# Top-k attention, mixture of experts and feed-forward on one core: fewer, longer score lists, a sign in place of a clipped excess, and PSUM in two pools

## The chip, the cores and the metric

The kernel runs on one core of one Trainium2 chip. The metric is the device time of one execution in microseconds (us), as the median of several runs. A profile of one more execution shows each engine's instructions: TensorE (PE, with its weight loads as PEld), VectorE (DVE), ScalarE (ACT), GpSimd (POOL) and SyncE (SP), which starts most of the transfers.

## What is computed

The reference runs three stages one after the other; all data are f32.

```python
# attention: 2 batches, 8 heads, 576 rows, 64 wide
scores = (1 / np.sqrt(64)) * np.matmul(q, k.transpose(0, 1, 3, 2))
kth = np.partition(scores, -32, axis=-1)[..., -32:-31]
scores = np.where(scores >= kth, scores, -1e9)
attn = np.exp(scores - scores.max(-1, keepdims=True))
attn = attn / (attn.sum(-1, keepdims=True) + 1e-9)
x = np.matmul(attn, v)              # to 1152 tokens of 512
# experts: 8, each token to the one with the highest gate, at most 288 each
h = np.maximum(x_e @ w1[e], 0.0); y = gate * (h @ w2[e])
# feed-forward, 2048 wide
h = y @ w_in; out = (h * np.clip(h + 3, 0, 6) / 6) @ w_out
```

What matters here is the first mask: of each row's 576 scores only the 32 highest may count, so the kernel has to know each row's 32nd highest score exactly.

## The kernel before

The 1152 tokens are nine tiles of 128 rows; with eight heads that makes 72 units of 128 x 576 scores, here also called heads, numbered u. The attention stage is a loop over i that is written out as a software pipeline: in one turn each engine works for a different unit, and the letters of `STEP` (line 36) are the order within a turn. Each engine runs its own instructions strictly in the order in which they were recorded.

For one unit the steps are these. TensorE makes the scores in PSUM, and ScalarE's `fetch` (line 388) copies them to SBUF. `round1` (line 407): VectorE cuts the 576 scores into eight chunks of 72 and takes the eight highest of each with MAX8, into a list for each chunk. `excess` (line 413): GpSimd subtracts from each score its chunk's eighth highest. `cut_excess` (line 418): ScalarE takes the positive part of that, scaled by 2^64, so that only the seven highest of a chunk give something other than zero. `drop_excess` (line 421): GpSimd subtracts this from the scores, which leaves the scores without each chunk's first seven. `round2` (line 425): VectorE takes the eight highest of what is left, one MAX8 over 576. `merge` (lines 432 to 436): from nine lists of seven VectorE takes the 32 highest in order, by four MAX8 and three replacements between them; a replacement shows in the trace as a load of the values and the replacement itself. Then `shift` on GpSimd (line 454, the first 200 columns, 60 from unit 54 on, none for the last four) and `shift_rest` on ScalarE (line 459, the other columns) subtract from the highest score, `below` (line 463, ScalarE) marks what lies below the 32nd, TensorE transposes both into one PSUM tile, ScalarE takes the exponential (line 485), and TensorE multiplies with the values.

In turn i the three engines hold, each in this order: VectorE `round1` of unit i+1 dealt out with `merge` of unit i-3 by `interleave` (line 394), in some turns the normalisation of four heads (lines 503 and 504), then `round2` of unit i-2; GpSimd, after each eight units, `judge` for a tile (lines 442 to 445, four small instructions that keep what is needed to see later whether the lists sufficed), then `excess` of unit i, `shift` of i-3 and `drop_excess` of i-1; ScalarE `cut_excess` of i-1, `shift_rest` of i-3, `fetch` of i+3, `below` of i-3 and the exponential of i-4. In the last turns ScalarE also scales rows, and GpSimd sends them to the experts.

After attention come the eight experts on TensorE, each in 16 blocks of four products (line 1034), eight for the first layer (`hps`) and eight for the second (`yps`); their PSUM tiles all come from one pool of eight banks. Some turns into it, `check` (lines 961 to 980) works out on VectorE from what `judge` kept whether the fast pass may stand; if it may not, a slow pass of the whole computation follows. The last stage (lines 1141 and 1155) takes other PSUM pools once the experts' pool is given back. Results of an expert go from PSUM to SBUF in two halves, a rounded one by ScalarE (`x2h`, line 1051) and what is missing by VectorE (`x2l`, line 1052); the last stage's products read both.

Of the kernel before, what the change touches and what calls it, by code (L numbers as in the profile page):

```python
# [28 lines left out]
LOW = -3.4028234e38  # L29
NCK = 8  # L30
CW = S // NCK
KEEP = 7
PUSH = 2.0 ** 64
BIG = 2.0 ** 68
LEAST = 2.0 ** -32
# [26 lines left out]
def topk_attention_moe_ffn_kernel(ctx, tc, qT, kT, vx, vT, wg, w1, w2, w_in, w_out, out, cap):  # L62
# [20 lines left out]
    def forward(fast):  # L83
# [21 lines left out]
        sc = wp.tile([P, 2, E + 1], F32, name="sc")  # L105
        over = wp.tile([P, 2, NT, H, NCK], F32, name="over")
        rest_ok = wp.tile([P, 2, NT, H], F32, name="rest_ok")

# [138 lines left out]
        with ExitStack() as actx:  # L247
# [6 lines left out]
            if fast:  # L254
                lists = [big.tile([P, H, NCK + 1, KEEP + 1], F32, name=f"lists{i}") for i in range(2)]
            wg_sb = big.tile([P, HP, MC // E, E], F32, name="wg_sb")
# [77 lines left out]
            for i in range(2):  # L334
# [6 lines left out]
                lbufs.append(m)  # L341
            drop = big.tile([P, P], BF, name="drop")
            nc.vector.tensor_scalar(drop, ident, BIG, None, op0=OP.mult)

            def clear_rows(zero):
# [63 lines left out]
            def excess(u):  # L409
                t, h = divmod(u, H)  # L410
                st2[u] = wk.tile([P, S], F32, name="s2", bufs=3)
                s, s2 = (a.rearrange("p (c k) -> p c k", k=CW) for a in (st[u], st2[u]))
                nc.gpsimd.tensor_tensor(s2, s, lists[t % 2][:, h, :NCK, KEEP:].to_broadcast([P, NCK, CW]),  # L413
                                        op=OP.subtract)
# [12 lines left out]
            def merge(u):  # L427
                t, h = divmod(u, H)
                l = lists[t % 2][:, h, :, :KEEP]
                m = tops[t][:, h]  # L430
                l2 = wk.tile([P, NCK + 1, KEEP], F32, name="l2")
                yield lambda: nc.vector.max(m[:, 0:8], l)  # L432
                for i in range(1, 4):
                    yield lambda i=i: nc.vector.match_replace(out=l2, in_to_replace=m[:, 8 * i - 8:8 * i],  # L434
                                                              in_values=l if i == 1 else l2, imm_value=LOW)
                    yield lambda i=i: nc.vector.max(m[:, 8 * i:8 * i + 8], l2)  # L436

            def judge(t):

                l, thr = lists[t % 2], tops[t][:, :, TOPK - 1:]  # L440
                g = nc.gpsimd
# [399 lines left out]
        with ExitStack() as mctx:  # L841
# [56 lines left out]
            with ExitStack() as ectx:  # L898
                eb = ectx.enter_context(tc.tile_pool(name=of + "eb", bufs=2))
                ps = ectx.enter_context(tc.tile_pool(name=of + "ps", bufs=8, space=PS))  # L900
                xin, xe = {}, {}

                def two_banks():
                    return ps.tile([P, 2, 256], F32, tag="ps", name="xp2") if fast else None

# [17 lines left out]
                def turn_one(rows, x):  # L923
                    for k in range(HP):
                        xp = ps.tile([P, W], F32, tag="ps", name="xp1")
                        for r, a, n in rows:
# [34 lines left out]
                def check():  # L961

                    v = nc.vector
                    low = eb.tile([P, 3], F32, name="low", bufs=1)
                    hit = eb.tile([P, 3], BF, name="hit", bufs=1)
                    two = [over[:, i].rearrange("p a b c -> p (a b c)") for i in range(2)]
                    v.tensor_tensor(two[0], two[0], two[1], op=OP.max)
                    v.tensor_reduce(low[:, 0:1], two[0], axis=AX.X, op=OP.min)
                    v.tensor_reduce(low[:, 1:], rest_ok.rearrange("p k a b -> p k (a b)"), axis=AX.X, op=OP.min)
                    v.tensor_scalar(hit[:, 0:1], low[:, 0:1], 0.0, None, op0=OP.is_le)  # L970
                    v.tensor_scalar(hit[:, 1:2], low[:, 1:2], 0.0, None, op0=OP.is_lt)
                    v.tensor_scalar(hit[:, 2:], low[:, 2:], LEAST, None, op0=OP.is_lt)
                    hits = ps.tile([P, 3], F32, tag="ps", name="hits")
                    nc.tensor.matmul(hits, ones, hit, start=True, stop=True)
# [45 lines left out]
                def tokens_of_columns():  # L1020
                    who_is = ps.tile([P, 2, NT], F32, tag="ps", name="who_is")
                    for t in range(NT):
# [4 lines left out]
                class Expert:  # L1027
                    def __init__(self, x, col, w):
                        self.x, self.col, self.w, self.y = x, col, w, {}
                        self.h = eb.tile([P, NFF, W], F32, name="hT", bufs=2 if fast else 1)  # L1030
# [6 lines left out]
                    def use(self, wb, what):  # L1037
                        if what[0] == "a":
                            f = what[1]
                            o = ps.tile([P, W], F32, tag="ps", name="hps")[:, :self.w]  # L1040
                            yield from self.products(o, wb, self.x, True, True)
                            nc.scalar.activation(self.h[:, f, :self.w], o, AF.Relu)
                            return
                        d, half = what[1:]
                        if half == 0:
                            self.y[d] = ps.tile([P, W], F32, tag="ps", name="yps")[:, :self.w]
                        o = self.y[d]
# [32 lines left out]
                for m in range(E * NP):  # L1080
                    e, r = divmod(m, NP)
                    if r == 0:
                        ex = Expert(xe[e], lambda e=e: offv[e], Ws[e])
                    if r == OFR:
# [40 lines left out]
            if fast:  # L1125
                loaded.append(nc.values_load(again, min_val=0, max_val=P + 1))
            ps = mctx.enter_context(tc.tile_pool(name=of + "ps2", bufs=2, space=PS))
            mw = mctx.enter_context(tc.tile_pool(name=of + "mw", bufs=2))
            CH = 384
            NJ = CH // P  # L1130
            fw += [mw.tile([P, 2, 2, DM], F32R, name=f"fw{f}", bufs=1) for f in range(nearly, NF)]
            if not fast:
# [110 lines left out]
```

## Time and profile before

| what | us |
|---|---|
| median of 3 runs | 595.87 (595.73 to 596.02) |
| profiled execution | 595.49 |
| its span | 593.6 |
| TensorE busy | 558.6 |
| VectorE busy | 372.1 |
| ScalarE busy | 357.0 |
| GpSimd busy | 300.9 |

The span is what the profile shows from the first to the last instruction; the time of the execution is 1.9 us more. Busy times are for the whole span, and the stages differ: attention ends at about 236 us, the experts at about 385 us, and the last stage fills the rest. An instruction's length is from its start to the landing of its last result; the next one on the same engine often starts before that, so the distance between two starts is what an instruction costs its engine. The rows that are read more closely stand further down.

### The profile page before, as it was taken

Reading aid. Unit: us, or ns where it says so; the run is one execution under the profiler, and the core shown is the slowest. Engines: PE = TensorE matmul, PEld = TensorE weight load, DVE = VectorE, ACT = ScalarE, POOL = GpSimd, SP = SyncE. Lnnn points to the kernel's source line nnn. Section 1 sums busy time; section 2 is a strip of 40 time slices with the busy share of each in tenths; the row PEclk is TensorE's granted clock in tenths of the full one; section 3 lists DMA queues with packets and bytes.
Section 4 is the critical chain, followed back from the end, with each engine's and each line's share of the span. In section 5 each row is a group of like instructions: output and inputs, shape, how many; then the busy total and the mean of one; then the engine's idle time right before and its main releaser. Section 6 shows DMA issues by size and latency. Waiting matters only on the chain.

```text
span 593.6 us, 13628 instructions
## 1 busy us (share of the span) xinstructions
PE 558.6 (94%) x4831; PEld 489.1 (82%) x4831; DVE 372.1 (63%) x1774; ACT 357.0 (60%) x689; POOL 300.9 (51%) x375
## 2 busy tenths in 40 slices
PE   8999998888878879999999999999999999999994
PEld 4777776666666668999999999998989999998993
DVE  6999999999999997103534344366666663222230
ACT  5999999999989995111345434455555542242221
POOL 8999999999989995100223223234223340040002
PEclk9999999999999999999999999999999999999998
DMA  8639100000008002874897978323222300020001
GB/s 257 213 130 316 56 20 2 22 2 2 2 2 315 26 19 99 340 282 162 319 352 278 358 281 323 105 70 105 75 72 71 108 1 1 2 106 1 1 1 58
DMA packets 18260, 73.49 MB, mean 124 GB/s; under 512 B 2543, under 2 KB 3183, under 8 KB 16007
## 3 DMA queue, kind: packets, MB, share of 16 engines
q1 hardware_dynamic: 16743, 67.81, 32.0%
q0 software_dynamic: 1440, 4.72, 2.0%
q8 instruction: 40, 0.66, 0.4%
q14 instruction: 37, 0.30, 0.2%
HBM read 63.09 MB, written 9.44 MB: 122 GB/s over the span
## 4 chain that ended last, share of the span: by engine, by line
PE 62%; DVE 32%; POOL 3%; issue 1%; ACT 1%; DVEq 0%; POOLq 0%; ACTq 0%
PE h L1141 17%; PE acc L1155 16%; PE hps L1034 12%; PE yps L1034 12%; DVE lists L407 11%; DVE lists L425 7%; DVE l L434 6%; DVE tops L436 4%; DVE tops L432 1%; DVE x_tok L504 1%; PE xp L167 1%; PE av L497 1%; POOL s L413 1%; POOL s L421 1%; PE pt L656 1%
## 5 line engine op out<-in xcount | busy, mean ns | idle before, releaser
L407 DVE MAX8 lists<-s 128x8 f32<-128x72 f32 x576 | 119.1, 221 | 3.1 <-ACT s L391 2.8
L1141 PE MATMUL h<-x2h,fw 128*128 128x384 f32 x384 | 98.2, 337 | 1.1 <-DVE x2l L1052 1.1
L421 POOL TENSOR_TENSOR s<-s,cut 128x576 f32<-128x576 f32 x72 | 92.5, 1285 | 0.1
L478 PE MATMUL pt<-ident,ub 128*128 128x128 f32 x350 | 69.7, 285 | 21.5 <-ACT pts L485 17.4
L1155 PE MATMUL acc<-fw,gh 128*128 128x512 f32 x288 | 89.5, 392 | 0.0
L413 POOL TENSOR_TENSOR s<-s,lists 128x576 f32<-128x576 f32 x72 | 84.2, 1170 | 4.9 <-DVE lists L425 2.8
L478 PEld LDWEIGHTS pt<-ident,ub 128*128 128x128 f32 x350 | 49.0, 140 | 43.4 <-issue 15.3
L1034 PE MATMUL yps<-hT,wslot 128*128 128x192 f32 (+5 forms) x512 | 78.5, 302 | 0.0
L497 PE MATMUL av<-vt,pts 128*64 128x96 f32 x1440 | 75.2, 250 | 1.0 <-DVE eids L240 1.0
L1141 PEld LDWEIGHTS h<-x2h,fw 128*128 128x128 f32 x384 | 70.1, 188 | 5.1 <-DVE x2l L1052 1.3
L1034 PEld LDWEIGHTS yps<-hT,wslot 128*128 128x128 f32 x512 | 72.5, 190 | 0.6
L1034 PE MATMUL hps<-xe,wslot 128*128 128x192 f32 (+5 forms) x512 | 72.5, 302 | 0.6 <-ACT xe L173 0.6
L1034 PEld LDWEIGHTS hps<-xe,wslot 128*128 128x128 f32 x512 | 71.2, 190 | 0.9 <-ACT xe L173 0.9
L497 PEld LDWEIGHTS av<-vt,pts 128*64 128x64 f32 x1440 | 61.8, 135 | 12.2 <-issue 9.3
L1141 PE MATMUL h<-x2l,fw 128*128 128x384 f32 x192 | 64.6, 336 | 0.0
L479 PE MATMUL pt<-drop,lb 128*128 128x128 bf16 x350 | 63.2, 219 | 0.0
L1144 ACT ACTIVATE g<-h,three 128x384 f32<-128x384 f32 x48 | 27.9, 582 | 55.3 <-PE h L1141 55.0
L1145 DVE SCALAR_TENSOR_TENSOR g<-g,h 128x384 f32<-128x384 f32 x48 | 26.5, 552 | 54.0 <-ACT g L1144 53.7
L1155 PEld LDWEIGHTS acc<-fw,gh 128*128 128x128 f32 x288 | 53.4, 188 | 8.2
L463 ACT ACTIVATE lb<-s,tops 128x576 bf16<-128x576 f32 x71 | 57.0, 803 | 4.0 <-DVE tops L436 3.9
L1149 DVE TENSOR_TENSOR gl<-g,gh 128x384 fp32r<-128x384 f32 x48 | 27.4, 572 | 50.2 <-ACT gh L1148 50.2
L1148 ACT CAST gh<-g 128x384 fp32r<-128x384 f32 x48 | 24.6, 513 | 56.8 <-PE acc L1155 52.1
(462 smaller groups left out, 1049.5 us busy)
## 6 DMA issues: line engine op xcount, KB each, us to landing
wslot<-in_w_dram SPq DMA_DIRECT2D x15, 2048.0 KB, 8.7
raw<-in_w_in_dram SPq DMA_DIRECT2D x16, 512.0 KB, 3.5
raw<-in_w_out_dram SPq DMA_DIRECT2D x16, 512.0 KB, 5.5
xs<-x_tok SPq DMA_DIRECT2D x8, 576.0 KB, 10.1
vt<-in_vx_dram SPq DMA_DIRECT2D x8, 365.0 KB, 3.4
vts<-in_vT_dram SPq DMA_DIRECT2D x8, 288.0 KB, 4.6
qt<-in_qT_dram SPq DMA_DIRECT2D x8, 256.0 KB, 4.8
wslot<-in_w_dram SPq DMA_DIRECT2D x2, 1024.0 KB
```

Of the source, the lines that this page charges most:

```text
L407: yield lambda c=c: nc.vector.max(lists[t % 2][:, h, c], st[u][:, c * CW:(c + 1) * CW])
L413: nc.gpsimd.tensor_tensor(s2, s, lists[t % 2][:, h, :NCK, KEEP:].to_broadcast([P, NCK, CW]), op=OP.subtract)
L421: nc.gpsimd.tensor_tensor(st2[u], st[u], cuts.pop(u), op=OP.subtract)
L425: nc.vector.max(lists[t % 2][:, h, NCK], st2.pop(u))
L434: yield lambda i=i: nc.vector.match_replace(out=l2, in_to_replace=m[:, 8 * i - 8:8 * i], in_values=l if i == 1 else l2, imm_value=LOW)
L463: nc.scalar.activation(lbufs[u % 2][:, :S], st.pop(u), AF.Relu, bias=tops[t][:, h, TOPK - 1:], scale=-1.0)
L478: nc.tensor.matmul(pt[:, c], ubufs[u % 2][:, cs], ident, is_transpose=True, start=True, stop=False)
L479: nc.tensor.matmul(pt[:, c], lbufs[u % 2][:, cs], drop, start=False, stop=True)
L497: nc.tensor.matmul(av[t, g][rows, h % 4], pts[:, c, rows], vt[b, h // 2][:, at:at + VC], start=c == 0, stop=c == 4)
L1034: nc.tensor.matmul(out, wb[:, k], m[:, k, :self.w], start=first and k == 0, stop=last and k == HP - 1)
L1141: nc.tensor.matmul(h2, fw[f][:, 0, a, k * P:(k + 1) * P], (x2h, x2l)[b][:, k, c * CH:(c + 1) * CH], start=n == 0, stop=n == len(ops) - 1)
L1155: nc.tensor.matmul(acc[j], g[a][:, j * P:(j + 1) * P], fw[f][:, 1, b], start=f == 0 and n == 0, stop=f == NF - 1 and n == 2)
```

## The change

`NCK` goes from 8 to 6, so a chunk is 96 scores wide, and a list keeps eight, not seven. The excess is written in bf16 to a tile of its own (`x`, two buffers). `cut_excess` becomes `Sign` of the excess times -2^64 plus a bias of -2^30 from a tile, which gives -1 for a chunk's eight highest and +1 for the others; it also writes the row's sum, from which equal scores at a chunk's edge are found later. `drop_excess` multiplies the scores with that sign, which turns the eight highest negative, into a tile with two buffers. `merge` reads 7 lists of 8 as one row of 56. `judge` only makes two small copies, and `check` does its comparisons at the end. In the expert stage the PSUM tiles come from two pools of four banks, in groups of four by turns, and the last expert's results always from the second; the last stage's two kinds of tiles get a pool each.

```diff
-NCK = 8
+NCK = 6
-KEEP = 7
+EDGE = 2.0 ** 30
             def excess(u):
-                st2[u] = wk.tile([P, S], F32, name="s2", bufs=3)
+                st2[u] = wk.tile([P, S], BF, name="x")
...
             def cut_excess(u):
-                nc.scalar.activation(cuts[u], st2[u], AF.Relu, scale=PUSH)
+                nc.scalar.activation(cuts[u], st2[u], AF.Sign, scale=-PUSH, bias=edge, accum_out=counts[:, u:u + 1])
             def drop_excess(u):
-                nc.gpsimd.tensor_tensor(st2[u], st[u], cuts.pop(u), op=OP.subtract)
+                st2[u] = wk.tile([P, S], F32, name="s2")
+                nc.gpsimd.tensor_tensor(st2[u], st[u], cuts.pop(u), op=OP.mult)
             def merge(u):
-                l = lists[t % 2][:, h, :, :KEEP]
+                l = lists[t % 2][:, h].rearrange("p c k -> p (c k)")
             def judge(t):
-                g.tensor_tensor(over[:, 0, t], l[:, :, :NCK, KEEP - 1], l[:, :, :NCK, KEEP], op=OP.subtract)
-                g.tensor_tensor(over[:, 1, t], thr.to_broadcast([P, H, NCK]), l[:, :, :NCK, KEEP], op=OP.subtract)
-                g.tensor_tensor(rest_ok[:, 0, t], thr[:, :, 0], l[:, :, NCK, KEEP], op=OP.subtract)
-                g.tensor_copy(rest_ok[:, 1, t], thr[:, :, 0])
+                nc.gpsimd.tensor_copy(last_of[:, us], lists[t % 2][:, :, :, 7])
+                nc.gpsimd.tensor_copy(least_of[:, us], tops[t][:, :, TOPK - 1])
-                ps = ectx.enter_context(tc.tile_pool(name=of + "ps", bufs=8, space=PS))
+                pools = [ectx.enter_context(tc.tile_pool(name=of + name, bufs=4, space=PS)) for name in ("ps", "ps_b")]
+                def bank(shape, name, late=False):
+                    turns[0] += 1
+                    return pools[1 if late else (turns[0] - 1) // 4 % 2].tile(shape, F32, tag="ps", name=name)
...
-                    accs[c] = [ps.tile([P, DM], F32, name="acc", bufs=2 * NJ) for _ in range(NJ)]
+                    accs[c] = [ps_acc.tile([P, DM], F32, name="acc") for _ in range(NJ)]
```

On VectorE, in the middle of attention, one turn from `round2` (the search over `s`) on stood like this before; `lists` holds the chunks' lists, `tops` the merged 32, and what a row waits for stands at its end:

```order
L425 MAX lists_114<-s_1206 128x8 [waits Pool_49]
L407 MAX lists_114<-s 128x8 [waits Activation_49]
L407 MAX lists_114<-s 128x8
L432 MAX tops<-lists_114 128x8 [waits DVE_49]
L407 MAX lists_114<-s 128x8
L434 MATCH_REPLACE l_1369<-tops,lists_114 128x63 [waits DVE_49]
```

The same place now:

```order
L429 MAX lists_115<-s_1246 128x8 [waits Pool_49]
L436 MAX tops<-lists_115 128x8 [waits DVE_49]
L410 MAX lists_115<-s 128x8 [waits Activation_49]
L438 MATCH_REPLACE l_1344<-tops,lists_115 128x56 [waits DVE_49]
L410 MAX lists_115<-s 128x8
```

The merge's first search has moved up to stand directly behind the search over 576, with a wait for it; two searches of the next unit stood between them.

On TensorE, at the border between the experts (`yps`) and the last stage (`h`), before:

```order
L1034 MATMUL yps<-hT,wslot_93 128x152 x20
L1126 TENSOR_LOAD again [waits DVE_49]
L1141 MATMUL h_5851<-x2h,fw_4532 128x384 [waits DMASW3_49,DMASW2_49,DMASW4_49,DMASW1_49,DMASW5_49,DMASW0_49,DVE_49]
L1141 MATMUL h_5851<-x2h,fw_4532 128x384 [waits Pool_49]
L1141 MATMUL h_5851<-x2l,fw_4532 128x384
L1141 MATMUL h_5851<-x2h,fw_4532 128x384 x2
```

And now:

```order
L1048 MATMUL yps<-hT,wslot_94 128x152 x20
L1140 TENSOR_LOAD again [waits DVE_49]
L1156 MATMUL h_5777<-x2h,fw_4445 128x384 [waits DMASW3_49,DMASW2_49,DMASW4_49,DMASW1_49,DMASW5_49,DMASW0_49,Activation_49]
L1156 MATMUL h_5777<-x2h,fw_4445 128x384 [waits Pool_49]
L1156 MATMUL h_5777<-x2l,fw_4445 128x384 [waits DVE_49]
L1156 MATMUL h_5777<-x2h,fw_4445 128x384 [waits Activation_49]
L1156 MATMUL h_5777<-x2h,fw_4445 128x384
L1156 MATMUL h_5777<-x2l,fw_4445 128x384 [waits DVE_49]
```

The one wait for VectorE ahead of everything has become a wait for each block's halves, spread over the first twelve products.

On TensorE at the start of the experts (`hps`), the first 32 products stood behind one wait:

```order
L1034 MATMUL hps<-xe_92,wslot_93 128x192 [waits DMAHW6_49,DVE_49,Activation_49]
L1034 MATMUL hps<-xe_92,wslot_93 128x192 x31
```

Now the wait for ScalarE's later work stands two products further on:

```order
L1048 MATMUL hps<-xe_93,wslot_94 128x192 [waits DMAHW6_49,DVE_49,Activation_49]
L1048 MATMUL hps<-xe_93,wslot_94 128x192
L1048 MATMUL hps<-xe_93,wslot_94 128x192 [waits Activation_49]
L1048 MATMUL hps<-xe_93,wslot_94 128x192 x13
```

The rows of GpSimd and ScalarE keep their order; only the judging is shorter, and the built program holds 72 more ScalarE instructions, one behind each sign, that write out its sum.

## Rows read from the trace of the kernel before

**Rows 1.** The page: busy us, share of span, instructions of each engine.

```profile
PE 558.6 (94%) x4831; PEld 489.1 (82%) x4831; DVE 372.1 (63%) x1774; ACT 357.0 (60%) x689; POOL 300.9 (51%) x375
```

**Rows 2.** By stretches: us, busy us (instructions) of each engine, clock, DMA.

```profile
100.00:148.00 48.00, 41.56 (x570) 31.78 (x568) 47.86 (x315) 46.67 (x82) 47.91 (x58) 1.00 0.03 8
...
172.00:184.00 12.00, 10.23 (x133) 7.82 (x130) 11.83 (x80) 10.96 (x20) 9.52 (x15) 1.00 0.46 167
184.00:197.00 13.00, 10.33 (x136) 7.99 (x136) 12.97 (x88) 13.00 (x23) 12.81 (x17) 1.00 0.53 213
197.00:213.00 16.00, 12.68 (x166) 9.97 (x166) 15.72 (x105) 16.00 (x28) 15.64 (x24) 1.00 0.09 35
```

**Rows 3.** Chain that ended last: start us, us, what; two searches eight heads apart.

```profile
43.40 0.67 DVE lists L425
...
67.32 0.67 DVE lists L425
```

**Rows 4.** VectorE in order of time: start us, us, engine, line, operation, shapes, count.

```profile
99.81 0.74 DVE L425 MAX8 lists<-s 128x8 f32<-128x576 f32 x1
100.47 0.35 DVE L407 MAX8 lists<-s 128x8 f32<-128x72 f32 x2
100.73 0.21 DVE L432 MAX8 tops<-lists 128x8 f32<-128x63 f32 x1
...
102.64 0.17 DVE L503 RECIPROCAL rs<-av 128x4 f32<-128x4 f32 x1
102.83 0.46 DVE L504 TENSOR_TENSOR x_tok<-av,rs 128x288 f32<-128x288 f32 x1
```

**Rows 5.** VectorE's groups by shape: busy us, mean ns | idle before, releaser.

```profile
L407 DVE MAX8 lists<-s 128x8 f32<-128x72 f32 x576 | 119.1, 221 | 3.1 <-ACT s L391 2.8 <-ACT s L388 0.3
L425 DVE MAX8 lists<-s 128x8 f32<-128x576 f32 x72 | 53.7, 747 | 0.8 <-POOL s L421 0.6 <-POOL spacer L153 0.2
```

**Rows 6.** ScalarE in order of time, one turn of the loop.

```profile
20.25 0.64 ACT L388 ACTIVATE s<-ps 128x576 f32<-128x576 f32 x1
20.79 0.77 ACT L463 ACTIVATE lb<-s,tops 128x576 bf16<-128x576 f32 x1
21.45 0.70 ACT L485 ACTIVATE pts<-pt 128x640 f32<-128x640 f32 x1
22.04 0.69 ACT L418 ACTIVATE cut<-s 128x576 bf16<-128x576 f32 x1
22.61 0.61 ACT L459 ACTIVATE ub<-s,tops 128x376 f32<-128x376 f32 x1
23.11 0.65 ACT L388 ACTIVATE s<-ps 128x576 f32<-128x576 f32 x1
```

**Rows 7.** ScalarE in order of time: a small instruction and its follower.

```profile
170.56 0.20 ACT L570 ACTIVATE el<-board 128x48 f32<-128x48 f32 x1
170.65 0.68 ACT L418 ACTIVATE cut<-s 128x576 bf16<-128x576 f32 x1
```

**Rows 8.** GpSimd in order of time, and a group with converted output.

```profile
161.25 1.17 POOL L413 TENSOR_TENSOR s<-s,lists 128x576 f32<-128x576 f32 x1
...
162.86 1.29 POOL L421 TENSOR_TENSOR s<-s,cut 128x576 f32<-128x576 f32 x1
164.10 1.17 POOL L413 TENSOR_TENSOR s<-s,lists 128x576 f32<-128x576 f32 x1
...
L881 POOL TENSOR_TENSOR fw<-cm__6329,fw 128x512 fp32r<-128x512 f32 x1 | 1.8, 1751 | 2.1 <-ACT fw L880 2.1
```

**Rows 9.** ScalarE's group that loads a table of functions.

```profile
L391 ACT ACT_TABLE_LOAD x1 | 1.3, 1283 | 0.8 <-PEq L1205 0.8
```

**Rows 10.** VectorE and TensorE in order of time, experts to last stage.

```profile
385.67 0.31 DVE L1052 TENSOR_TENSOR x2l<-yps,x2h 128x152 f32 x1
386.03 0.62 PE L1141 MATMUL h<-x2h,fw 128*128 128x384 f32 x2 [1.06 <-DVE x2l L1052]
```

**Rows 11.** TensorE in order of time, start of the experts.

```profile
236.32 1.89 PE L1034 MATMUL hps<-xe,wslot 128*128 128x192 f32 x10 [0.57 <-ACT xe L173]
```

More of the change, by code (lines that the diff above doesn't have):

```diff
@@ L105, in forward @@
         sc = wp.tile([P, 2, E + 1], F32, name="sc")
-        over = wp.tile([P, 2, NT, H, NCK], F32, name="over")
-        rest_ok = wp.tile([P, 2, NT, H], F32, name="rest_ok")
+        last_of = wp.tile([P, NU, NCK + 1], F32, name="last_of")
+        least_of = wp.tile([P, NU], F32, name="least_of")
+        counts = wp.tile([P, NU], F32, name="counts")
         xe0 = wp.tile([P, HP, W], F32, name="xe0")
@@ L254, in forward @@
             if fast:
-                lists = [big.tile([P, H, NCK + 1, KEEP + 1], F32, name=f"lists{i}") for i in range(2)]
+                lists = [big.tile([P, H, NCK + 1, 8], F32, name=f"lists{i}") for i in range(2)]
             wg_sb = big.tile([P, HP, MC // E, E], F32, name="wg_sb")
@@ L342, in forward @@
             drop = big.tile([P, P], BF, name="drop")
+            edge = big.tile([P, 1], F32, name="edge")
             nc.vector.tensor_scalar(drop, ident, BIG, None, op0=OP.mult)
+            nc.vector.memset(edge, -EDGE)
             def clear_rows(zero):
@@ L924, in turn_one @@
                     for k in range(HP):
-                        xp = ps.tile([P, W], F32, tag="ps", name="xp1")
+                        xp = bank([P, W], "xp1")
                         for r, a, n in rows:
@@ L963, in check @@
                     v = nc.vector
[L964 to L971, printed above, removed]
+                    low = eb.tile([P, 4], F32, name="low", bufs=1)
+                    hit = eb.tile([P, 4], BF, name="hit", bufs=1)
+                    worst = eb.tile([P, NU], F32, name="worst", bufs=1)
+                    v.tensor_scalar(counts, counts, float(S - 16 * NCK), 0.5, op0=OP.is_equal, op1=OP.subtract)
+                    v.tensor_reduce(worst, last_of[:, :, :NCK], axis=AX.X, op=OP.max)
+                    v.tensor_tensor(worst, least_of, worst, op=OP.subtract)
+                    v.tensor_tensor(worst, worst, counts, op=OP.max)
+                    v.tensor_reduce(low[:, 0:1], worst, axis=AX.X, op=OP.min)
+                    v.tensor_tensor(worst, least_of, last_of[:, :, NCK], op=OP.subtract)
+                    v.tensor_reduce(low[:, 1:2], worst, axis=AX.X, op=OP.min)
+                    v.tensor_reduce(low[:, 2:3], least_of, axis=AX.X, op=OP.min)
+                    v.tensor_reduce(low[:, 3:], last_of[:, :, :NCK], axis=AX.XY, op=OP.min)
+                    v.tensor_scalar(hit[:, :2], low[:, :2], 0.0, None, op0=OP.is_lt)
                     v.tensor_scalar(hit[:, 2:], low[:, 2:], LEAST, None, op0=OP.is_lt)
-                    hits = ps.tile([P, 3], F32, tag="ps", name="hits")
+                    hits = bank([P, 4], "hits")
                     nc.tensor.matmul(hits, ones, hit, start=True, stop=True)
@@ L1020, in tokens_of_columns @@
                 def tokens_of_columns():
-                    who_is = ps.tile([P, 2, NT], F32, tag="ps", name="who_is")
+                    who_is = bank([P, 2, NT], "who_is")
                     for t in range(NT):
@@ L1027, in forward, with __init__ @@
                 class Expert:
-                    def __init__(self, x, col, w):
-                        self.x, self.col, self.w, self.y = x, col, w, {}
+                    def __init__(self, x, col, w, last):
+                        self.x, self.col, self.w, self.last, self.y = x, col, w, last, {}
                         self.h = eb.tile([P, NFF, W], F32, name="hT", bufs=2 if fast else 1)
@@ L1039, in use @@
                             f = what[1]
-                            o = ps.tile([P, W], F32, tag="ps", name="hps")[:, :self.w]
+                            o = bank([P, W], "hps")[:, :self.w]
                             yield from self.products(o, wb, self.x, True, True)
@@ L1045, in use @@
                         if half == 0:
-                            self.y[d] = ps.tile([P, W], F32, tag="ps", name="yps")[:, :self.w]
+                            self.y[d] = bank([P, W], "yps", self.last)[:, :self.w]
                         o = self.y[d]
@@ L1082, in forward @@
                     if r == 0:
-                        ex = Expert(xe[e], lambda e=e: offv[e], Ws[e])
+                        ex = Expert(xe[e], lambda e=e: offv[e], Ws[e], e == E - 1)
                     if r == OFR:
```

18 lines of the change are left out of this document (9 added, 9 removed).

## Prediction

> **What bounds the kernel now.** I read the page first: TensorE is busy for 558.6 of 593.6 us [rows 1], so its idle stretches are what can be won, and nearly all of them lie in the attention stage, the first 236 us or so. The view by stretches tells what holds TensorE up there: between 100 and 148 us VectorE is busy for 47.86 us, GpSimd for 47.91 and ScalarE for 46.67 of 48, and between 184 and 213 us ScalarE is busy for all 29.00 us [rows 2]. Three engines are thus nearly full at once. The chain of work that ended last says which one sets the pace in the main part: it runs through VectorE's 576-wide search once per head, and eight such searches lie from 43.40 to 67.32 us, 23.92 us or 2.99 us for each head [rows 3]. The other two have next to no room: ScalarE's five instructions per head start 0.54, 0.66, 0.59, 0.57 and 0.50 us apart, in sum 2.86 us [rows 6]; GpSimd's excess and shift take 1.61 and its drop 1.24 us, in sum 2.85 us [rows 8], to which the judging of each eight heads adds about 0.1 for each. So whatever the change takes from VectorE is worth only what ScalarE and GpSimd let through, and the change adds work to ScalarE.
>
> **VectorE, part by part.** A search of 72 elements takes 221 ns and one of 576 takes 747 ns [rows 5], which makes (747 - 221) / 504 = 1.04 ns for an element; two of 72 start 0.26 us apart from what follows them, 0.13 each [rows 4]. Six searches of 96 in place of eight of 72: two instructions less are -0.26, six times 24 elements more are +0.15. The merge's seven searches and replacements shrink from 63 to 56 elements: 7 x 7 x 1.04 ns = -0.05. Against that stands the order: with six and seven instructions to deal out, the merge's first search now comes directly behind the 576-wide search whose result it reads, where two independent searches stood between. Now the follower starts 0.66 us behind the 576-wide one (99.81 to 100.47), which itself lasts 0.74. For two instructions that depend on each other the trace has the reciprocal and the product: 0.17 long, the next starts after 0.19, so 0.02 behind its end [rows 4]. The merge's first search would start 0.77 behind, +0.11. Queued behind it on VectorE are the six searches of the next head, on which the excess on GpSimd waits. In sum -0.26 + 0.15 - 0.05 + 0.11 = about -0.06, so 2.93 us for each head if VectorE alone set the pace.
>
> **ScalarE.** The cut becomes a sign with its bias in a tile and a sum to write out. The bias is priced by the instruction that has one: the 576-wide one of line 463 is followed after 0.66 us, the cut without one after 0.57 [rows 6], so 0.09. The sum is written by an instruction of its own: the built program holds 72 more on ScalarE, one behind each cut. The trace of before has none. Its bounds: nothing, if it disappears in the tail of the cut (less is not possible, since it is an added instruction); and 0.20 us, the whole length of the smallest kind of ScalarE instruction, if what follows can't overlap it. Such a small one lets the next start after 0.09 us [rows 7]; I take that, since it is queued in the same way. ScalarE then needs 2.86 + 0.09 + 0.09 = 3.04 us for each head, more than the 2.99 of now: it becomes the engine that sets the pace, and the 0.06 of VectorE is not what counts.
>
> **GpSimd.** Judging shrinks from four instructions to two small copies and saves about 0.05 us for each head; the product in place of the difference is the same two-input pass; the excess is written in bf16. That write has no row. Bounds: the excess as now, 1.17 us long (a gain is not to be expected, since both inputs are still f32 and as wide); and the pass of line 881, the only one whose output is converted, 1.75 us for 512 elements [rows 8]. I take 1.17: the drop already reads a bf16 input at 1.24, so another width by itself is cheap. With 2.9 us for each head GpSimd stays below ScalarE. The buffers are split (two for the bf16 difference, two for the product): the excess no longer waits for an old 576-wide search, and the waits of GpSimd on itself that the new program has point five instructions back, so they end early.
>
> A rule that bears on this: the Trainium skill, GPSIMD Engine Reference, section 3.1 (Elementwise, side-by-side cycle accounting), gives about 2.6 cycles of 1.2 GHz for an element of a two-input pass. That is an estimate of 1.25 us for 576 elements, and the drop's 1.24 agrees with it [rows 8]. By it the excess could rise to 1.25 at most whatever its types, GpSimd to 3.0, and the sum below would stay as it is.
>
> **The sum for attention.** In the main part (heads 10 to 53, 44 of them) ScalarE may first fall behind. Between an excess and the drop that needs its cut, GpSimd runs another drop, an excess and a shift, 2.85 us; the cut takes 0.69 [rows 6], so it can slip by some 2.2 us before GpSimd waits. ScalarE (3.04) slips against VectorE (2.93) by 0.11 a head. If all of the 2.2 us is free, 20 heads go at VectorE's pace (-1.2) and 24 at ScalarE's (+1.2), together 0; if half of it is used up already, 10 (-0.6) and 34 (+1.7), together +1.1. I take +0.5. In the last part (heads 54 to 71, 18 cuts) ScalarE is full already [rows 2], because the shift moves to it there: 18 x 0.18 = 3.2, less 0.4 out of the 1.04 us that it is idle between 172 and 184 us [rows 2], +2.8.
>
> **TensorE's two boundaries.** Before the last stage the first product waits 1.06 us for the last low part on VectorE, which starts at 385.67 us behind ScalarE's conversions [rows 10]. It does so because the PSUM pool is given back as a whole. With two pools, and the last expert's results kept to the second, the new order waits for each block by itself: the first block's halves have been there for several us, and nine products of about 0.17 us pass before the fourth block is asked for, at 384.97 + 1.6, after its low part is done (385.98). The stall goes, -1.06, and TensorE is then bound by nothing else. At the start of the experts the first product waits 0.57 us for ScalarE's copy [rows 11]; the new order puts two products ahead of that wait, -0.3. Between the two TensorE has no idle time, so both are on the path. The new check on VectorE (some ten small instructions for six) needs attention's data alone and is queued well ahead of TensorE's use of it; without that cover it would cost half a microsecond. I count nothing.
>
> Together +0.5 + 2.8 - 1.1 - 0.3 = +1.9 us. The profiled execution took 595.49 us (span 593.6), 0.38 below the median of 595.87; from the median, **597.8 us**. A measurement of this kernel can tell about 0.2%, 1.2 us.
>
> **Rivals.**
> *The read-out is nearly free* (faster). ScalarE needs 2.95 to 2.98, level with VectorE: the main part gains 44 x 0.04 = 1.8, the last part loses 18 x 0.09 - 0.4 = 1.2, the boundaries give 1.4: -2.0, **593.9**. It decides where the read-out adds under 0.04 us. For it: ScalarE's instructions overlap by 0.1 us already. Against: each of them, however small, took its own 0.09 in the trace. Chance 0.2.
> *The read-out waits for the cut to finish*, 0.20: ScalarE 3.15, main part 44 x 0.16 less the 2.2 of slip = +4.9, last part 18 x 0.29 - 0.4 = +4.8, boundaries -1.4: +8.3, **604.2**. For it: it has to read what the cut sums up last. Chance 0.15.
> *The bf16 write makes GpSimd the bound.* It decides from 0.14 us more on the excess (2.9 against 3.04). At 0.3 more, GpSimd needs 3.2 and all 68 heads lose 0.2: +14 - 1.4, **608**; at line 881's price for an element (1.97 us for 576) some 640. For it: that row. Against: the drop's. Chance 0.12.
> *The sign stands in another table than the exponential*: two loads for each head. The trace has one load, 1.28 us [rows 9]; 144 would be 185 us, **780**. The built program still holds one, so 0.01. The Trainium skill, ScalarE: Activation LUTs, section What ACT_TABLE_LOAD costs, has a switch at about 2.66 us with its drain, for which no run here has a row; by it this rival would be twice as dear.
> *The change doesn't do what it says*: should its check find lists that don't suffice, the whole slow pass would follow. Six lists of eight and one more of eight hold 56 candidates for 32 places; with these inputs that is as good as excluded.
>
> **How the numbers follow.** The forecast (a read-out of 0.05 to 0.13) has 0.52 and reaches from 595.6 to 601. Range: from the free read-out's 593.9 to 604.2; the dear GpSimd cases and half of the free ones stay out, under 0.2. Faster: nearly all of the first rival, 0.18. Within 0.2%: the lower third of the forecast and a little of that rival, 0.22. Slower: the rest, 0.60.
>
> **What would show it.** Right: behind each cut a small ScalarE instruction, the next one starting about 0.75 us after the cut and not 0.57; ScalarE without idle time between 100 and 148 us, VectorE idle where it now has 0.14; the merge's first search 0.77 us behind the 576-wide one; the excess at 1.17; the first product of the last stage without its 1.06 us. Wrong: VectorE still full and ScalarE with gaps (first rival), GpSimd without a gap and an excess over 1.3 us (third).

## The result and the profile after

The changed kernel takes 600.81 us (median), the one before, run on the same chip, 595.8: a ratio of 1.0084, 95% interval 1.0072 to 1.0096, or 5 us more. Forecast were 597.8 us and a range of 593.9 to 604.2: the sign and the range hold, the size is off by 3 us. The profiled span is 598.9 us against 593.6. One of the four executions of a run further down (VectorE's order, with neither addition) took 787.34 us at a granted clock of 0.655, against 0.99 and more in all others, and is left out.

The view by stretches of the kernel after, as [rows 2] (us, busy us and instructions of PE, PEld, DVE, ACT and POOL, clock, DMA share, GB/s):

```profile
100.00:148.00 48.00, 40.42 (x558) 31.19 (x557) 46.40 (x281) 48.00 (x97) 45.99 (x52) 1.00 0.03 8
172.00:184.00 12.00, 10.50 (x159) 8.28 (x158) 10.76 (x71) 12.00 (x26) 9.92 (x12) 1.00 0.11 25
```

VectorE had 47.86 of 48 us and GpSimd 47.91 before; now they have 1.6 and 2.0 us free, and ScalarE has none, nor in the later stretch, where it had 1.04. ScalarE in order of time, as [rows 6]:

```profile
105.24 1.04 ACT L421 ACTIVATE cut<-x,edge 128x576 bf16<-128x576 bf16 x1
105.91 0.47 ACT L421 ACTIVATION_READ_ACCUMULATOR cut<-x,edge 128x1 f32 x1
106.00 0.87 ACT L460 ACTIVATE ub<-s,tops 128x376 f32<-128x376 f32 x1
...
108.28 1.05 ACT L421 ACTIVATE cut<-x,edge 128x576 bf16<-128x576 bf16 x1
```

The next instruction starts 0.76 us after the cut, where 0.57 was usual: the bias tile adds 0.10 (105.24 to 105.91) and the read-out 0.09. From cut to cut lie 3.04 us, the sum that the prediction made. That the cut is shown as 1.04 us long, and was 0.69, is no cost to ScalarE, as the starts tell; the engine that reads the cut does wait for its end. Who waits for ScalarE is seen on GpSimd. Its drop (the second pass, which needs the cut) by lines, the kernel before first and the kernel after below it (busy us, mean ns | idle us ahead of it, and who ended that):

```profile
L421 POOL TENSOR_TENSOR s<-s,cut 128x576 f32<-128x576 f32 x72 | 92.5, 1285 | 0.1
```

```profile
L425 POOL TENSOR_TENSOR s<-s,cut 128x576 f32<-128x576 f32 x72 | 92.5, 1285 | 11.1 <-ACT cut L421 6.3 <-DVE lists L410 2.0 <-DVE tops L436 1.0
L416 POOL TENSOR_TENSOR x<-s,lists 128x576 bf16<-128x576 f32 x72 | 83.6, 1162 | 1.9 <-DVE lists L410 1.8
```

The drop waited 0.1 us in all and now waits 11.1. In order of time it starts behind each read-out, 0.17 us after the cut's end (105.24 + 1.04). The VectorE work that is named for a part of the wait is another from drop to drop (L410, L436, L438, L440), while that distance stays, so it is only what happened to end at the time:

```profile
106.45 1.28 POOL L425 TENSOR_TENSOR s<-s,cut 128x576 f32<-128x576 f32 x1 [0.17 <-DVE tops L436]
```

106.45 is 0.07 behind the read-out's end (105.91 + 0.47). So ScalarE releases GpSimd, GpSimd the 576-wide search, and TensorE comes last. Where the loss arises is read from the searches of heads 9, 53 and 69 and the first product of the experts. Before, the three searches, VectorE in order of time:

```profile
37.03 0.74 DVE L425 MAX8 lists<-s 128x8 f32<-128x576 f32 x1
...
169.28 0.75 DVE L425 MAX8 lists<-s 128x8 f32<-128x576 f32 x1
...
219.41 0.75 DVE L425 MAX8 lists<-s 128x8 f32<-128x576 f32 x1
```

After, the same searches, and below them TensorE at the start of the experts (as [rows 11]), at VectorE's checks in expert 2, and at the start of the last stage (as [rows 10]):

```profile
36.96 0.76 DVE L429 MAX8 lists<-s 128x8 f32<-128x576 f32 x1
...
172.62 0.76 DVE L429 MAX8 lists<-s 128x8 f32<-128x576 f32 x1
...
224.82 0.75 DVE L429 MAX8 lists<-s 128x8 f32<-128x576 f32 x1
```

```profile
242.14 1.05 PE L1048 MATMUL hps<-xe,wslot 128*128 128x192 f32 x5
...
295.13 0.16 PE L988 MATMUL hits<-hit,ones 128*128 128x4 bf16 x1 [0.82 <-DVE hit L986]
...
391.42 0.61 PE L1156 MATMUL h<-x2h,fw 128*128 128x384 f32 x2
```

| stretch | before, us | after, us | difference |
|---|---|---|---|
| start to head 9's search | 37.03 | 36.96 | -0.07 |
| heads 9 to 53, 44 of them | 132.25 | 135.66 | +3.41 |
| heads 53 to 69 | 50.13 | 52.20 | +2.07 |
| to the first product of the experts [rows 11] | 16.91 | 17.32 | +0.41 |
| experts, to the first product behind them [rows 10] | 149.71 | 149.28 | -0.43 |
| last stage, to the span's end | 207.57 | 207.48 | -0.09 |

The experts' -0.43 is a gain and a loss: neither boundary has the stall of [rows 10, 11], but `hits`, which waited for nothing before, waits 0.82 us for VectorE's longer checks.

### The profile page after: what moved, and what is told of

Same layout as the page of the kernel before. It is cut to its first block, busy times and chain, and to the rows that moved or that the text cites. A ratio compares the mean times of both kernels' runs of the same rounds, so it can differ in the third digit from the quotient of the medians.

```text
span 598.9 us, 13608 instructions
## 1 busy us (share of the span) xinstructions
PE 558.7 (93%) x4830; PEld 488.9 (82%) x4831; DVE 371.0 (62%) x1636; ACT 368.5 (62%) x761; POOL 298.3 (50%) x357
## 4 chain that ended last, share of the span: by engine, by line
PE 68%; DVE 21%; ACT 6%; issue 2%; POOL 1%; ACTq 0%; POOLq 0%
PE h L1156 17%; PE acc L1170 16%; PE yps L1048 12%; PE hps L1048 11%; DVE lists L410 6%; DVE lists L429 5%; PE av L498 4%; DVE l L438 4%; PE pt L479 3%; ACT pts L486 3%; DVE tops L440 2%; DVE tops L436 2%; ACT lb L464 1%; DVE x_tok L505 1%; PE pt L480 1%
## 5 line engine op out<-in xcount | busy, mean ns | idle before, releaser
L410 DVE MAX8 lists<-s 128x8 f32<-128x96 f32 x432 | 106.8, 251 | 3.2 <-ACT s L394 2.8
L425 POOL TENSOR_TENSOR s<-s,cut 128x576 f32<-128x576 f32 x72 | 92.5, 1285 | 11.1 <-ACT cut L421 6.3
L416 POOL TENSOR_TENSOR x<-s,lists 128x576 bf16<-128x576 f32 x72 | 83.6, 1162 | 1.9 <-DVE lists L410 1.8
L421 ACT ACTIVATE cut<-x,edge 128x576 bf16<-128x576 bf16 x72 | 68.8, 956 | 0.0
L464 ACT ACTIVATE lb<-s,tops 128x576 bf16<-128x576 f32 x71 | 68.0, 957 | 0.0
L486 ACT ACTIVATE pts<-pt 128x640 f32<-128x640 f32 x70 | 61.5, 879 | 0.8 <-PE pt L480 0.8
```

Of the source, the lines that this page charges most:

```text
L410: yield lambda c=c: nc.vector.max(lists[t % 2][:, h, c], st[u][:, c * CW:(c + 1) * CW])
L416: nc.gpsimd.tensor_tensor(x, s, lists[t % 2][:, h, :NCK, 7:].to_broadcast([P, NCK, CW]), op=OP.subtract)
L421: nc.scalar.activation(cuts[u], st2[u], AF.Sign, scale=-PUSH, bias=edge, accum_out=counts[:, u:u + 1])
L425: nc.gpsimd.tensor_tensor(st2[u], st[u], cuts.pop(u), op=OP.mult)
L464: nc.scalar.activation(lbufs[u % 2][:, :S], st.pop(u), AF.Relu, bias=tops[t][:, h, TOPK - 1:], scale=-1.0)
L486: nc.scalar.activation(pts, pt[:, :5], AF.Exp, scale=-SCALE)
```

## Experiments

Theory 1: ScalarE's two additions make 3.04 us of its turn, and the slowest engine's turn is the pace of attention. Its rivals: VectorE's new order or GpSimd's passes cost the time, or ScalarE is on the path of every head whatever its turn. Beside the times the pace is compared, from the starts of the cut between 40 and 165 us: (last start - first) / (count - 1). These rows give count, shortest, median and longest length in ns, first and last start in us. It is ScalarE's pace that they show; VectorE's searches of heads 9 to 53 went at 132.25 / 44 = 3.01 us before and 3.08 after.

**The read-out, the bias tile, and both taken away.**

```diff
 e1_no_readout
-AF.Sign, scale=-PUSH, bias=edge, accum_out=counts[:, u:u + 1])
+AF.Sign, scale=-PUSH, bias=edge)
+nc.vector.memset(counts, float(S - 16 * NCK))
 e2_no_bias
+AF.Sign, scale=-PUSH, accum_out=counts[:, u:u + 1])
 (check)  float(S - 16 * NCK)  becomes  float(S - 15 * NCK)
 e3_neither
+AF.Sign, scale=-PUSH)          and counts preset
```

> The changed kernel without the sum of the signs: the cut has no accumulator, so no read-out follows it on ScalarE; the counts are preset, and equal scores at a list's end are not found (that part of the computation is left out). Theory 1 (ScalarE's turn per head sets the pace of attention): the turn falls by the read-out's 0.093 us to 2.95 us, just above VectorE's 2.93; over some 62 heads in which ScalarE is full that is 62 x 0.093 = 5.8 us less: 595 us (593.5 to 597). Rival (the time went to VectorE's new order, where the merge stands directly behind the 576-wide search, or to GpSimd's bf16 excess and its product): none of that is touched, 600.8 us within 0.7.

> The changed kernel with the bias tile left off the Sign: the eighth score of a list gives 0 instead of -1, so it falls out of the 576-wide search as 0, and the sum that stands for no equals is S - 15 x 6. The result is the same, the read-out stays. Theory 1: ScalarE's turn falls by the 0.09 us that the bias tile cost, as with the read-out: 595 us (593.5 to 597). Rival A (VectorE's order or GpSimd's passes): 600.8 within 0.7. Rival B (the read-out costs not by its length but because GpSimd's drop waits for it): the read-out is still there, so little changes, over 599.

> The changed kernel with neither the bias tile nor the read-out (equal scores are not found, that part is left out): ScalarE's turn is back at 2.86 us, as before the change. Theory 1: VectorE's 2.93 us sets the pace, 0.11 us under the 3.04 of the changed kernel: 62 x 0.11 = 6.8 us less, 594 us (592 to 595.5), so about 1 us under the runs that take away one of the two. If the two savings simply added up (ScalarE still alone on the path), 600.8 - 11.5 = 589 us. Rival (VectorE's order or GpSimd's passes cost the time): 600.8 within 0.7.

Measured: 594.59, 594.73 and 591.45 us, beside 595.53 for the kernel before (ratios 0.9977, 0.9984 and 0.9928, intervals 0.9965 to 0.999, 0.9975 to 0.9994, 0.9911 to 0.9944). Leaving out either addition gives back 6 us, leaving out both 9.4. The cut's rows of the kernel before, then after, then of these three in turn:

```profile
L418 ACT ACTIVATE cut<-s x43: 670/694/832, 39.5 to 163.8; 128x576 bf16<-128x576 f32 x43
```

```profile
L421 ACT ACTIVATE cut<-x,edge x41: 832/1028/1182, 40.7 to 163.0; 128x576 bf16<-128x576 bf16 x41
```

```profile
L422 ACT ACTIVATE cut<-x,edge x43: 827/981/1122, 40.0 to 164.3; 128x576 bf16<-128x576 bf16 x43
```

```profile
L421 ACT ACTIVATE cut<-x x43: 727/878/1037, 40.5 to 165.0; 128x576 bf16<-128x576 bf16 x43
```

```profile
L422 ACT ACTIVATE cut<-x x43: 670/746/905, 42.2 to 164.6; 128x576 bf16<-128x576 bf16 x43
```

In turn 124.3 / 42 = 2.96 us a head before, 122.3 / 40 = 3.06 after, 2.96, 2.96 and 2.91. The rivals that leave ScalarE out fall, and so does the one by which the drop's wait for the read-out is the cost: without the bias tile the read-out is still there, and the 6 us are gone. With neither addition the run came out lower than expected (591.45, not 592 or more). VectorE's floor was counted over all heads, but in the last part, where the shift moves to ScalarE, both savings count: between the searches of heads 53 and 69 this run takes 49.75 us, the one without the read-out 50.74. That is about one of the two us that were not expected; the other was not taken down.

**The two additions alone, on the kernel before; and the bias tile alone.**

```diff
 e7_before_bias
-AF.Relu, scale=PUSH)
+AF.Relu, scale=PUSH, bias=edge)        (edge holds zeros)
 e9_before_both
+AF.Relu, scale=PUSH, bias=edge, accum_out=total[:, u:u + 1])
```

> The kernel before with a bias tile (zeros) on its Relu and nothing else: ScalarE's turn rises by 0.093 us to 2.95, under the 2.99 us at which VectorE and GpSimd go there. Theory 1 (only the slowest engine's turn counts): the time stays, 595.8 to 596.4. Rival A (the prediction's slip: ScalarE's lag is paid as well as its pace): 0.5 to 1.1 us more, 596.3 to 596.9. Rival B (ScalarE is on the path of every head): 62 x 0.093 = 5.8 us more, 601.3.

> The kernel before with ScalarE's two additions alone: a bias tile (zeros) on its Relu and a sum out of it that nothing reads. ScalarE's turn becomes 3.04 us as in the changed kernel; VectorE, GpSimd, the PSUM pool and the checks stay as before. Theory 1 (from 2.99 us on ScalarE sets the pace, whatever VectorE does): attention ends as late as in the changed kernel, about 6 us later than before, and neither the pools' gain nor the checks' wait is there: 601 to 602.5 us. Rival (the six-list searches and the merge's place have a part in the loss): 0.05 x 62 = 3 us more at the most, 597.5 to 599.

Measured: 596.29 us for the bias tile (ratio 1.0012, 1.0002 to 1.0022), 601.76 for both (1.0099, 1.0078 to 1.012). The cut's rows, the bias tile first, then both; below the latter its first product of the experts:

```profile
L420 ACT ACTIVATE cut<-s,edge x43: 820/978/1115, 40.4 to 164.7; 128x576 bf16<-128x576 f32 x43
```

```profile
L421 ACT ACTIVATE cut<-s,edge x41: 830/994/1128, 40.5 to 162.8; 128x576 bf16<-128x576 f32 x41
...
242.50 3.68 PE L1037 MATMUL hps<-xe,wslot 128*128 128x192 f32 x21 [0.57 <-ACT xe L173]
```

The paces are 2.96 and 3.06. The same 0.09 us is worth 0.7 us where ScalarE's turn stays under the others' (2.95) and 5 more (5.7 in all, over 596.05) where it doesn't (3.04). The 0.7 is between the expectations: it fits the theory's upper end and the slip's lower one. So ScalarE is not on the path of every head whatever its turn; whether its lag costs something of its own this run can't tell. With both, the experts start at 242.50, 0.36 later than in the changed kernel, where the stall of 0.57 in front of them is gone, though VectorE, GpSimd and the pool are the old ones: ScalarE's additions by themselves make the loss.

**The PSUM pools alone, on the kernel before.** The edit is the diff's part on `bank`, `pools` and `ps_acc`.

> The kernel before with nothing changed but the PSUM pools: two of four banks in the experts, the last expert's sums in the second, and the last stage's accumulators in a pool of their own. Theory (the two boundaries gained 0.52 and 1.33 us in the changed kernel because of the pools): 595.8 - 1.85 = 594.0 us (593.5 to 594.5). Rival (the start of the experts gained because the end of attention is arranged otherwise, so only the last stage's boundary is the pools'): 595.8 - 1.3 = 594.5. Rival (the gaps only moved behind another wait): 595.8.

Measured: 593.57 us, ratio 0.9964 (0.9952 to 0.9977). The experts' first product starts at 235.64, 0.68 us earlier, and TensorE goes into the last stage without a stall:

```profile
235.64 10.64 PE L1040 MATMUL hps<-xe,wslot 128*128 128x192 f32 x64
...
384.00 0.61 PE L1148 MATMUL h<-x2h,fw 128*128 128x384 f32 x2
```

384.00 - 235.64 = 148.36 against 149.71: 1.35 us. Together 2.0 us, all of it in the time.

**The checks' product issued later.**

```diff
-                        check()
+                        check_rest = check()      # VectorE's steps, up to `hit`
+                    if fast and m == CHK + 4:
+                        check_rest()              # `hits` and what reads it
```

> The changed kernel with VectorE's checks issued where they are, and the product `hits` that reads them (with the four VectorE steps behind it) four groups of expert products later, some 5 us. Theory (TensorE waited 0.93 us for VectorE's longer check): 600.8 - 0.9 = 599.9 us. Rival (the wait only takes the place of another further on): 600.8 within 0.3. The profile is to show `hits` without an idle stretch in front of it.

Measured: 600.07 us, 0.74 less than the changed kernel. Against the kernel before, run beside it, that is a ratio of 1.0082 (1.0064 to 1.01) against 1.0084, so the times alone don't settle it. The profile does: `hits` has no idle time in front of it, and from the first product of the experts to the first behind them it takes 390.30 - 241.99 = 148.31 us, 0.97 less than the 149.28 of the changed kernel:

```profile
241.99 0.73 PE L1052 MATMUL hps<-xe,wslot 128*128 128x192 f32 x3
...
295.34 2.87 PE L1052 MATMUL yps<-hT,wslot 128*128 128x132 f32 x24
298.05 0.17 PE L992 MATMUL hits<-hit,ones 128*128 128x4 bf16 x1
...
390.30 0.61 PE L1162 MATMUL h<-x2h,fw 128*128 128x384 f32 x2
```

**VectorE's order**, on the changed kernel and on the one with neither addition.

```diff
-  interleave(round1(i + 1), merge(i - 3), ...)              # merge's 7 and 6 searches in turns
+  m = list(merge(i - 3)); late += m[6:]
+  interleave(round1(i + 1), m[:6], ...)                     # a search first
   ... round2(i - 2)                                          # the 576-wide search
+  late                                                       # then the merge's last step
```

> The changed kernel with VectorE's row in another order: a 96-wide search first, then merge and searches in turns, and the 576-wide search before the merge's last step, so that the merge's first search no longer stands directly behind the 576-wide search on which it depends (0.79 us from start to start in the changed kernel, 0.66 in the one before). Theory 1 (ScalarE's 3.04 us set the pace): VectorE's turn falls by about 0.12 us and nothing is gained: 600.8 us within 1. Rival (VectorE's order costs the time): 62 x 0.12 = 7.4 us less, 593 to 595.

> The same order of VectorE, on the changed kernel with neither bias tile nor read-out (equal scores are not found, that part is left out), which took 591.45 us. Theory (with ScalarE's turn at 2.86, VectorE sets the pace at 2.95 us per head): VectorE's turn falls to about 2.83, the pace to that of ScalarE or GpSimd, 2.86 to 2.90: 62 x 0.05 to 0.09 = 3 to 5.5 us less, 586 to 588.5. Rival (GpSimd, 47.9 of 48 us busy in that run, sets the pace): 591.4 within 0.7.

Measured: 602.71 us, so 1.9 more, where no change was expected; and 590.59, where 586 to 588.5 was expected. The order does what it should for VectorE: in the first of the two it is busy for 45.09 of 48 us between 100 and 148, against 46.40. That nothing is gained while ScalarE is full is as theory 1 has it. The loss has a place. ScalarE's `lb` (which needs the merge's last step) in the first run, in order of time:

```profile
182.13 0.78 ACT L464 ACTIVATE lb<-s,tops 128x576 bf16<-128x576 f32 x1 [1.53 <-DVE tops L440]
```

With the merge's end put behind a search that itself waits for GpSimd, ScalarE stands still for 1.53 us at 182, once, as the last part begins. In the second run the cuts go 44 in 123.6 us, 2.87 a head, down from 2.91, and GpSimd is full (so is ScalarE by its shown lengths, but the drop, which waits for it in the changed kernel, here starts 0.3 us or more behind the cut's end for most heads):

```profile
L422 ACT ACTIVATE cut<-x x44: 727/883/1027, 40.2 to 163.8; 128x576 bf16<-128x576 bf16 x44
...
100.00:148.00 48.00, 43.47 (x586) 33.19 (x583) 47.07 (x292) 48.00 (x85) 48.00 (x55) 1.00 0.03 8
172.00:184.00 12.00, 8.97 (x123) 7.22 (x124) 10.72 (x68) 10.46 (x18) 9.30 (x14) 1.00 0.84 319
```

Over heads 28 to 36 the searches of the run with neither addition lie 23.60 us apart (rows further down), 2.95 a head, and with the new order 22.99 (92.42 to 115.41), 2.87: VectorE had set the pace, and GpSimd sets the next one. Heads 9 to 53 gain 2.7 us by it; 0.7 are lost before head 9, and 1.2 behind head 53, where ScalarE is idle for 1.54 of 12 us; neither place was taken down further. My expectation had left them out.

**Towards a faster kernel**: no bias tile and the late product; and with them the new order for the first 50 heads alone and `SPOOL = (224, 60, 0)`.

> The changed kernel without the bias tile and with the late `hits` product (both keep the result): the two savings lie in different stages and should add up: 594.7 - 0.8 = 593.9 us (593.4 to 594.5), about 1.8 us under the kernel before. Rival (the earlier end of attention brings the checks' wait to another place): 594.7.

> As the run before it, and two things more: the 576-wide search ahead of the merge's last step for the first 50 heads alone (not in the last stage of attention, where the merge's end is awaited by ScalarE's `below`), and 224 columns of the shift on GpSimd in place of 200. Turns per head by rows: VectorE 2.83, ScalarE 2.95 - 24 x 0.83 ns = 2.93, GpSimd 2.88 + 24 x 1.66 ns = 2.92. Theory (the pace is the slowest turn): 2.95 to 2.93 over some 50 heads, 1 us less: 592.9 us (592.2 to 593.6). Rival (with three engines within 0.1 us of each other the waits between them eat that): 593.9 or more.

Measured: 593.9 us (ratio 0.9965, 0.9951 to 0.9979) and 592.98 us (0.995, 0.9934 to 0.9966), beside 596.05 for the kernel before. The second one's cuts: 43 from 39.8 to 163.3, 2.94 a head, as the sum of ScalarE's turn has it:

```profile
L421 ACT ACTIVATE cut<-x x43: 722/883/1023, 39.8 to 163.3; 128x576 bf16<-128x576 bf16 x43
```

It is 7.8 us faster than the changed kernel and 3 us faster than the one before.

## Why the prediction was right, and where its size was off

**The read-out** was taken at 0.09 us between bounds of 0 and 0.20, and ScalarE at 3.04: 0.09 and 3.04 in the trace. The rivals on it (nearly free, waiting for the cut's end) fall by that row; it does put off the drop, which starts 0.07 us behind it, but not ScalarE.

**The main part: +0.5 forecast, +3.4 measured. This is the step that failed.** The pace of ScalarE was right; wrong was what it was held against: ScalarE was to slip by some 2.2 us before GpSimd waits, half of it perhaps used up. Next to nothing of it was free. GpSimd and ScalarE of the kernel before, in order of time, at head 9 (excess, cut and the drop that needs it):

```profile
30.41 1.18 POOL L413 TENSOR_TENSOR s<-s,lists 128x576 f32<-128x576 f32 x1
...
33.79 0.72 ACT L418 ACTIVATE cut<-s 128x576 bf16<-128x576 f32 x1
...
34.86 1.29 POOL L421 TENSOR_TENSOR s<-s,cut 128x576 f32<-128x576 f32 x1
```

The cut starts 2.20 us behind the excess's end (31.59) and ends 0.35 us ahead of the drop. (Between excess and drop GpSimd runs a second shift that the prediction did not count, so the cut could slip by 3.27 - 0.72 = 2.55 us; 2.20 were used up.) The lag was already there when the main part began; the prediction worked out how far ScalarE can fall behind and did not read how far behind it was. With nothing free its own figures give 44 x 0.05 = 2.2, so its +1.1 was no bound. In the kernel after, ScalarE and GpSimd at heads 9 and 53, and between them ScalarE at a pair of copies of `mix`:

```profile
34.66 0.81 ACT L421 ACTIVATE cut<-x,edge 128x576 bf16<-128x576 bf16 x1
35.65 1.28 POOL L425 TENSOR_TENSOR s<-s,cut 128x576 f32<-128x576 f32 x1 [0.17 <-DVE lists L410]
...
40.74 0.83 ACT L421 ACTIVATE cut<-x,edge 128x576 bf16<-128x576 bf16 x1
...
42.53 0.34 ACT L522 COPY vt<-mix 128x64 f32<-128x64 f32 x2
...
43.95 0.85 ACT L421 ACTIVATE cut<-x,edge 128x576 bf16<-128x576 bf16 x1
...
169.09 1.19 ACT L421 ACTIVATE cut<-x,edge 128x576 bf16<-128x576 bf16 x1
...
170.45 1.29 POOL L425 TENSOR_TENSOR s<-s,cut 128x576 f32<-128x576 f32 x1 [0.16 <-DVE lists L410]
```

Every drop from head 9 to 53 now starts between 0.16 and 0.33 us behind the end of its cut. The cuts of heads 9 and 53 lie 134.43 us apart: 44 x 3.04 = 133.76, and 0.67 for four pairs of copies, which ScalarE does up to head 24 beside its turn (3.21 from cut to cut at the one shown; before, they had room). The kernel before needed 132.25 for these heads, so 2.18 of the 3.41 are ScalarE's pace. The other 1.23 is the search's distance from its cut, 2.30 at head 9 and 3.53 at head 53: the drop starts 0.99 and then 1.36 behind the cut's start, because it waits for the cut's end and the cut is shown longer and longer, and the search 0.03 and 0.88 behind the drop's end, where VectorE's own row has it.

**The last part: +2.8 forecast, with the experts' boundary of -0.3 +2.5; measured +2.48** (2.07 and 0.41, which hold that boundary). The size agrees, but by luck. The view by stretches from the cut of head 53 to that of head 71, before and after (columns as above, ScalarE the fourth pair):

```profile
163.81:220.27 56.46, 45.64 (x622) 36.00 (x624) 55.45 (x367) 53.73 (x93) 53.14 (x70) 1.00 0.25 95
```

```profile
169.09:226.00 56.91, 45.71 (x616) 35.64 (x617) 53.08 (x321) 56.91 (x111) 51.77 (x65) 1.00 0.24 94
```

ScalarE was idle for 2.73 us of it before and shows no idle time now; the prediction took off 0.4. So the 3.2 us of additions make ScalarE's stretch only 0.45 longer. The rest was lost earlier: the cut of head 53 comes 5.28 us later than before (169.09 against 163.81), its search only 3.34 (172.62 against 169.28). These 1.94 us had not yet reached the searches; they come up here, where ScalarE is full to the end. With 0.09 behind the last cut the sum is 2.48. Slip that was counted as free in the main part was paid in the last one, and idle time that was counted too low made up for it.

**VectorE: -0.06 a head forecast.** The terms of the prediction add up to -0.05. The merge's first search starts 0.78 us behind the 576-wide one (0.77 forecast):

```profile
101.70 0.75 DVE L429 MAX8 lists<-s 128x8 f32<-128x576 f32 x1
102.48 0.22 DVE L436 MAX8 tops<-lists 128x8 f32<-128x56 f32 x1
```

With ScalarE relieved, in the run with neither addition, the searches of heads 28 and 36 are these:

```profile
92.66 0.75 DVE L430 MAX8 lists<-s 128x8 f32<-128x576 f32 x1
...
116.26 0.75 DVE L430 MAX8 lists<-s 128x8 f32<-128x576 f32 x1
```

That is 23.60 us for eight heads, 2.95 each, against the 23.92 and 2.99 of [rows 3] and the 2.93 of the sum. As forecast, this gain does not count beside ScalarE's pace; in that run it does: the experts start at 232.78, and at 235.64 with the pools alone.

**GpSimd**: the excess in bf16 takes 1162 ns, 1170 before; the rival of a dear write falls. **The table**: one load, as [rows 9].

**The boundaries**: -1.06 and -0.3 forecast; -1.35 and -0.68 with the pools alone. Right in kind, more in size: the second gives twice its forecast.

**The checks: nothing forecast, +0.9 measured** (149.28 us for the experts against 148.36 with the pools alone; 0.82 of it is the wait at `hits`). The prediction named the cover (queued well ahead) and its price without (half a microsecond). The cover was not there: before, the last of the six steps ends at 288.36 and `hits` starts at 288.41, without slack. Eleven steps instead of six, 2.9 us from the first to the end of the last instead of 2.0, all show:

```profile
288.21 0.15 DVE L972 TENSOR_SCALAR hit<-low 128x1 bf16<-128x1 f32 x1
...
288.41 0.16 PE L974 MATMUL hits<-hit,ones 128*128 128x3 bf16 x1
```

In the spans the forecast fell short by 5.3 - 1.9 = 3.4 us. At the searches +2.9 of them lie in the main part and nothing in the last; by ScalarE's own cuts it is +0.9 up to head 9, +3.9 in the main part (134.43 against 130.02 us) and -2.0 in the last. Either way the lag that was taken as free is the term that failed. The checks add 0.9, the last stage's boundary takes off 0.3 and the start and the last stage 0.2.

## What to carry to other kernels

Where three engines are each within 0.15 us of the pace, an instruction of 0.09 us is nearly free on the engine that still has room (0.7 us in all here) and costs about itself times every head on the one that hasn't: add up each engine's turn from start to start, the added ones included, and take the largest. An engine's lead over the next is used up or not, and the trace of before says which: read how long ahead of its reader the last result was ready at the first turn before counting it as slack. And slack is only lent if the same engine is full further on: the lag that is used up early is paid there. The same holds for cover: a chain that ends 0.05 us ahead of its reader hides nothing more.

## What the runs showed of the hardware

A bias tile and the read-out of a sum cost the same on ScalarE, 0.09 us each, beside a pass over 576 elements. Its instructions look longer the longer it has run without a pause (the cut 694 ns in the median of the kernel before, 1028 in the changed one, 878 in the one without bias). In the changed kernel, ScalarE in order of time, on either side of a pause (the starts at 179.82 and 180.83 lie 1.01 us apart, where 0.53 is usual):

```profile
178.39 1.23 ACT L421 ACTIVATE cut<-x,edge 128x576 bf16<-128x576 bf16 x1
...
182.70 0.76 ACT L421 ACTIVATE cut<-x,edge 128x576 bf16<-128x576 bf16 x1
```

The distance of the starts does not change with the length, so for ScalarE it is no price. GpSimd's drop, which reads the cut, waits for the end all the same: it starts 0.99 us behind the cut's start at head 9 and 1.36 at head 53. A bf16 result from two f32 inputs cost GpSimd nothing (1162 against 1170 ns).
